# An adaLN, linear attention and GEGLU kernel: 1/den loads of another shape, two modulation products at other places, and the down projection's pairs interleaved

## The chip, the cores and the metric

One core of one Trainium2 chip. The metric is the device time of one execution in microseconds, the median of several runs; lower is better.

## The reference

The computation, cut to what matters (S = 2048 rows, D = 1024, 32 heads of 32, F = 3584; inputs in bf16):

```python
mod = (silu(c) @ w_mod).reshape(1, 6, 1, D)
sa, ca, ga, sb, cb, gb = ...                     # six rows of D
h = layernorm(x) * (1 + ca) + sa
q, k, v = heads(h @ wqkv)                        # [heads, S, 32]
phi = lambda t: where(t > 0, t + 1, exp(t)) + 1e-6
pq, pk = phi(q), phi(k)
kv = einsum('hsd,hse->hde', pk, v)
z = einsum('hsd->hd', pk)
num = einsum('hqd,hde->hqe', pq, kv)
den = einsum('hqd,hd->hq', pq, z)[..., None] + 1e-6
x = x + ga * (rows(num / den) @ wo)
h = layernorm(x) * (1 + cb) + sb
x = x + gb * ((gelu(h @ w_gate) * (h @ w_up)) @ w_down)
```

## The kernel before

Rows of x come in 16 chunks of 128 (`NCH`), in four super-groups of four chunks (`sg`, 512 rows); columns in eight groups of 128 (`g`), each holding four heads (`HPG = 4`, index k in the loads below). Every engine has one list of operations. PE (TensorE) and SP (the engine that issues nearly all DMAs) run theirs as written in the code; between two marks, from the startup to the first chunks of the wo stage, a planner (`reorder`) sorts the lists of VectorE (DVE), ScalarE (ACT) and GpSimd (POOL) by costs and due times. Waits are placed from what each operation reads and writes. SP's DMAs go round robin over eight lanes, and each DMA waits for the one eight before it.

The stages, in the order of PE:

- To about 127 us: q and k of h = LN(x), and phi of both.
- 127 to 191 us: 24 **m tiles** (`m_tile`), three of 342 columns or less for each group g, form pk^T against h; their results are transposed by DMA (`m_t`, tiles mb to mtb, L703) and multiplied by wv (`kv_prod`, L913), which gives each head's kv. The table `HOOK` says what is put on PE and SP behind which tile: `modp` = `mod_pass` (the products that turn the rows of sb and cb into one row each, `mod_rows`, and their store and reload as the columns sbT and cbT), `den0` and `den1` = `den` (pq against z, two super-groups each, four matmuls of 32 columns side by side, L1240, then reciprocal and a store to DRAM), `w0`, `w1` = `w2_pair` (kv times wo, 64 x 64 tiles, L1201), `gbr` = `gb_rows` (the row of gb), `rb...` = `rb_load`, `ps...` = `pq_scale`.
- 191 to 257 us, the **wo stage**: for each chunk 16 matmuls of pq against W2 (L1283), then x + the result and the second layernorm; ln2's rows are transposed by DMA (`T2`).
- 241 to 603 us: the FFN's gate and up products in 28 units, by a seven-product (Strassen-Winograd) scheme; their result goes to DRAM (`scr_y`).
- 599 to 778 us: the **down projection**, eight pairs of chunks (`d_pair0`, `d_pair`) by the same scheme, and the tail.

**1/den.** `scr_rd` holds 1/den in DRAM as [sg, h, k, g, 256]: h is a half of 256 rows. `rb_load` (L1255 to L1264) spreads it over partitions into `RB[sg % 2]`, two buffers: partitions 32k to 32k + 31 get head k's values. For each (sg, h) it issues four DMAs, one for each k, each from one row of 8 KB, repeated for 32 partitions. `pq_scale` (L1269 to L1274) multiplies pq in place, two g at a time on DVE; each multiply waits for all four DMAs. The chunks of (sg, h) wait for their multiplies. rb0 is loaded behind m tile 17, rb2.0 behind tile 23, rb1 and rb2.1 at the start of the wo stage, rb3 between its chunks (the table `SLOT`).

**A pair of the down projection.** For chunks ca and ca + 1 the products P1 to P7 have 14 matmuls each. P1 and P2 take y (`ya`, loaded from `scr_y` by `y_in`, two DMAs for each pair) and w_down (`wd`) as they are, in bf16; the others take sums of y (`d_s`, written to `sb` on DVE) and of w_down (`d_t`, `dt`, `dh`), in fp32. A pair uses four PSUM banks b0 to b0 + 3, and pairs alternate between b0 = 0 and 4. `d_cp` and `d_ecp` copy a bank to another bank or to the tile `DE` (ACT); `d_add` adds `DE` to a bank (DVE); `evac` multiplies by gb, adds x (`xq`, loaded by `x_in`) and stores the output. `hooks(i)` places further loads and sums after the products. For pairs 1 to 7 the order is P1, P5, P6, P2, P7, P3, P4:

```python
for k in (1, 5, 6, 2, 7, 3, 4):
    ...
    d_prod(ca, b0, k)
    if k == 1:   d_cp(b0 + 2, b0, "dpcp")
    elif k == 5: d_ecp(b0 + 3); d_s(ca, 2)
    elif k == 6: d_add(b0 + 1, b0 + 2); d_s(ca, 3); y_next(0)
    elif k == 2: evac(*parts[0])
    elif k == 7: d_add(b0 + 3, b0 + 2); d_s(ca, 4); y_next(1); evac(*parts[3])
```

Of the kernel before, what the change touches and what calls it, by code (L numbers as in the profile page):

```python
# [8 lines left out]
ALU = mybir.AluOpType  # L9
# [321 lines left out]
def bass_adaLN_cond__linear_attn_block__geglu_ffn__prompt_kernel(  # L331
# [18 lines left out]
    with ExitStack() as es:  # L350
# [449 lines left out]

        def gb_hilo(j):
            acc, rng = GA_[j]
            sch.op(A, lambda e: e.activation(HLG[:, j, 0, :], acc[:, :], ACTF.Copy), rd=rng, wr=r_hlg(j, 0), note=f"mhi{6 + j}")
            sch.op(V, lambda e: e.tensor_tensor(HLG[:, j, 1, :], acc[:, :], HLG[:, j, 0, :], ALU.subtract), rd=rng + r_hlg(j, 0), wr=r_hlg(j, 1), note=f"mlo{6 + j}")
# [3 lines left out]
        def gb_rows():  # L808
            mod_rows(((0, 2, 5, lambda j, h: (HLG[:, j, h, :], r_hlg(j, h))),))
            o_gb[0] = mod_store(2, 5, MRG, [(OFF_TMP + 4096, OFF_TMP + 5120, "mrg")], 2)  # L810
# [384 lines left out]

        def w2_pair(i, b0=4):
            for hf in range(2):
                for r in range(2):
                    for h in range(2):
                        b, g = b0 + 2 * r + hf, 2 * i + h  # L1200
                        sch.op(T, lambda e, b=b, g=g, h=h, r=r, hf=hf: e.matmul(ps_all[64 * h:64 * h + 64, b * 512:(b + 1) * 512], KVT[64 * r:64 * r + 64, g, 0:64],  # L1201
                               WO[64 * r:64 * r + 64, g, hf * 512:(hf + 1) * 512], start=True, stop=True),
                               rd=r_kvt(g, g + 1) + r_wo(g, hf * 512, (hf + 1) * 512), pwr=pr(b), note=f"w2 {i}.{hf}", overwrite_ok=True)
            for r in range(2):
                b, g = b0 + 2 * r, 2 * i + r
                w_, p_ = W2[:, g, :], ps_all[:, b * 512:(b + 2) * 512]
                eng = V if i > 1 and r else A
                sch.op(eng, lambda e, w_=w_, p_=p_, eng=eng: e.activation(w_, p_, ACTF.Copy) if eng == A else e.tensor_copy(w_, p_),
                       prd=pr(b) + pr(b + 1), wr=r_w(OFF_WK, "w2", g), note=f"w2cp{g}")
# [15 lines left out]
        def mod_pass():  # L1225
            assert mdone[0] >= 48 and not late
            mod_rows(((2, 4, 5, hl_src),))
            o_r = mod_store(4, 5, MROW[1], r_2k(OFF_ROW + 2048, "mrow1"), 1)
            for dst, nt, a0 in ((SBT, "sbT", 0), (CBT, "cbT", 2)):
                sch.dma(Q, lambda e, dst=dst, a0=a0: e.dma_start(dst[:, :], scr_row[1, a0:a0 + 2, :].rearrange("a (b p) -> p (a b)", p=P)),  # L1230
                        wr=r_sm(nt), deps=[o_r], note=nt)
# [21 lines left out]
        rb_ops = {}  # L1253

        def rb_load(sg, hs=(0, 1)):  # L1255
            i = sg % 2
            for h in hs:
                made = []
                for k in range(HPG):
                    made.append(sch.dma(Q, lambda e, h=h, k=k: e.dma_start(  # L1260
                        RB[i][32 * k:32 * (k + 1), h, :, :].rearrange("p a b -> p (a b)"),
                        scr_rd[sg, h, k:k + 1, :, :].rearrange("k g t -> k (g t)").to_broadcast([32, NG * HW])),
                        wr=r_rb(i, h) if k == 0 else (), deps=made[0].deps if k else [o_rd[sg // 2]], note=f"rb{sg}.{h}.{k}"))
                rb_ops[sg, h] = made  # L1264
# [3 lines left out]
        def pq_scale(sg, h, gs):  # L1268
            i, t0 = sg % 2, h * HW  # L1269
            for g0, g1 in gs:  # L1270
                ap = PQ[sg][:, g0:g1, t0:t0 + HW]
                rng = r_pq(sg, g0, g1, t0, t0 + HW)
                sch.op(V, lambda e, ap=ap, i=i, h=h, g0=g0, g1=g1: e.tensor_tensor(ap, ap, RB[i][:, h, g0:g1, :], ALU.mult),
                       rd=rng + r_rb(i, h, g0, g1), wr=rng, deps=rb_ops[sg, h], note=f"pqs{sg}.{h}.{g0}")  # L1274
# [3 lines left out]
        def wo_mm(c_, b0, gs):  # L1278
# [9 lines left out]
            if gs[-1] == NG - 1:  # L1288
# [13 lines left out]
        HOOK = {0: "ga", 6: "kv0", 10: "kv1", 11: "w0", 13: "kv2", 15: "modp kv3 z32", 16: "den0", 17: "w1 rb0.0 rb0.1", 18: "",  # L1302
                19: "kv4", 20: "den1 ps0.0", 21: "gbr", 22: "ps0.1", 23: "rb2.0"}
        st = {}

        def hook_run(f):
            if f[:2] == "kv":
                kv_prod(int(f[2:]), 4)
            elif f == "ga":
                ga_pass()  # L1310
            elif f == "gbr":
                assert mdone[0] == 64
                gb_rows()
            elif f == "modp":
                mod_pass()
            elif f == "z32":
                z32()
            elif f[:3] == "den":
                st[int(f[3:])] = den(int(f[3:]), 5)
                st[int(f[3:])]()  # L1320
            elif f[:2] == "ps":
                pq_scale(int(f[2]), int(f[4]), GH[0] + GH[1])
            elif f[:2] == "rb":
                rb_load(int(f[2]), (int(f[4]),))
            elif f[0] == "w":
                w2_pair(int(f[1:]))
# [328 lines left out]
        def d_prod(ca, b0, k, own=None, js=None):  # L1655
            b = b0 + {1: 0, 2: 0, 5: 3, 6: 2, 7: 2, 4: 2, 3: 1}[k] if own is None else own
# [3 lines left out]
            for j in js:  # L1660
# [11 lines left out]
                o = sch.op(T, lambda e, l_=l_, r_=r_, j=j, dst=dst: e.matmul(dst, l_[:, 0, :], r_, start=(k in (1, 5) or own is not None) and j == js[0], stop=j == js[-1], skip_group_check=True),  # L1672
# [48 lines left out]

        def d_pair(i, hook):
# [8 lines left out]
            for k in (1, 5, 6, 2, 7, 3, 4):  # L1731
                if last and k == 3:
                    d_prod(ca, b0, 3, None, range(6, NDJ))
                    evac_part(*parts[1])
                    continue
                d_prod(ca, b0, k)
                if k == 1:
                    d_cp(b0 + 2, b0, "dpcp")
                elif k == 5:
                    d_ecp(b0 + 3)  # L1740
                    d_s(ca, 2)
                elif k == 6:
                    d_add(b0 + 1, b0 + 2)
                    d_s(ca, 3)
                    y_next(0)
                elif k == 2:
                    evac(*parts[0])
                elif k == 7:
                    d_add(b0 + 3, b0 + 2)
                    d_s(ca, 4)  # L1750
                    y_next(1)
                    evac(*parts[3])
# [131 lines left out]
        def hooks(i):  # L1884
            def hook(k):
                more = i + 1 < 2 * CPG
                if i == 1:
                    if k == 1:
                        d_t(2, 5)
                        d_t(2, 6)  # L1890
                    if k in (6, 2, 7):
                        d_t(4, {6: 4, 2: 5, 7: 6}[k])
                    if k in (6, 7):
                        n = 1 if k == 6 else 2
                        evac(*parts_of(0)[n])
                        x_in(1, n)
                else:
                    if k == 1:
                        x_in(i, 0, 3, 1)
                    elif k == 5:  # L1900
                        x_in(i, 2)
                    if not more and k in (5, 6):
                        for q in {5: (0, 1), 6: (2,)}[k]:
                            t_gb(q)
            return hook

        d_pair0(hook0)
        for i in range(1, 2 * CPG):
            d_pair(i, hooks(i))
# [75 lines left out]
```

## Time and profile before

| what | us |
|---|---|
| median of three runs (782.70 to 783.98) | 782.91 |
| span of the profiled execution | 780.9 |
| FFN units, one every | 12.56 |
| down projection, one pair after pair 0 every | 22.03 |

The granted TensorE clock is 1.00 in every slice. "L1283" is line 1283 of the kernel; a line of a group names engine, operation and tiles (result<-inputs); in the timelines the columns are start, duration, engine, line, operation, tiles, shape and count, and in brackets the idle time before and what ended it. PE's busy time counts matmuls; weight loads (PEld) run beside them. A DMA's issue is SP's time to hand it over; "us to landing" is the time from issue until all of it is there.

The page's list of DMA issues for the transfers that the change touches (KB each, median us from issue to landing):

```
ya<-scr_y SPq DMA_DIRECT2D x14, 896.0 KB, 4.9
rb<-scr_rd SPq DMA_DIRECT2D x32, 256.0 KB, 6.0
xq<-scr_x SPq DMA_DIRECT2D x32, 128.0 KB, 2.6
scr_rd<-rdc SPq DMA_DIRECT2D x2, 128.0 KB, 3.8
mtb<-mb SPq DMA_TRANSPOSE x8, 4.9
```

### The profile page before, as it was taken

The page shows a single profiled execution, that of the slowest core. Times are in us where ns is not written, and L with a number is a line of the kernel's source. Part 1 is how long each engine was busy: PE and PEld are TensorE (multiplying, and loading weights), DVE is VectorE, ACT ScalarE, POOL GpSimd, SP SyncE. Part 2 cuts the span into 40 slices and gives each one's busy share as a digit, 9 for nine tenths or more (in the row PEclk, how much of TensorE's full clock was granted, in tenths as well). Part 3 has the DMA queues.
Part 4 walks back from the last instruction along what each step waited for, and adds up shares of the span by engine and source line. Part 5 has one row for each costly group of instructions (what it writes and reads, how often), then busy time and mean ns, then how long its engine had stood idle before and what let it go on. Part 6 is the DMA issues. An engine that isn't in the chain of part 4 may idle for free.

```text
span 780.9 us, 10753 instructions
## 1 busy us (share of the span) xinstructions
PE 770.2 (99%) x3825; PEld 496.2 (64%) x3883; DVE 645.9 (83%) x964; ACT 374.6 (48%) x629; POOL 47.5 (6%) x126
## 2 busy tenths in 40 slices
PE   8999999999999999999999999999999999999998
PEld 4444445666445667667676767667676576677766
DVE  6699988897899878787989888888989888676767
ACT  2497743242466487878755555555555211111111
POOL 2031300000321011100000000000000000000000
PEclk9999999999999999999999999999999999999999
DMA  9879749939999358867353865535356334443331
GB/s 284 256 167 252 158 91 215 255 80 196 203 287 231 82 138 212 230 175 215 99 145 108 250 211 172 148 96 161 97 147 221 111 127 139 144 141 114 126 125 60
DMA packets 196940, 130.22 MB, mean 167 GB/s; under 512 B 69516, under 2 KB 182420, under 8 KB 195864
## 3 DMA queue, kind: packets, MB, share of 16 engines
q1 hardware_dynamic: 196872, 129.55, 62.4%
q8 instruction: 30, 0.49, 0.3%
q14 instruction: 22, 0.18, 0.1%
q10 hardware_dynamic: 16, 0.00, 0.0%
HBM read 92.55 MB, written 23.35 MB: 148 GB/s over the span
## 4 chain that ended last, share of the span: by engine, by line
PE 95%; SPq 2%; DMA 1%; DVE 1%; issue 1%; ACT 0%; DVEq 0%; ACTq 0%
PE ps_all L1458 45%; PE ps_all L1672 21%; PE ps_all L895 7%; PE ps_all L934 7%; PE ps_all L1283 7%; PE ps_all L880 5%; PE ps_all L1593 1%; SPq L598 1%; DMA wmq<-in_w_mod_dram 1%; SPq L603 1%; DMA h1T<-xh 0%; PE ps_all L913 0%; PE ps_all L1201 0%; PE ps_all L1240 0%; DVE h1T L724 0%
## 5 line engine op out<-in xcount | busy, mean ns | idle before, releaser
L1458 PE MATMUL ps_all<-ss,tp 128*128 128x512 f32 x896 | 214.3, 396 | 0.0
L1458 PEld LDWEIGHTS ps_all<-ss,tp 128*128 128x128 f32 x896 | 168.3, 188 | 37.8 <-DVE ss L1413 0.2
L1672 PE MATMUL ps_all<-dt,sb 128*128 128x512 f32 x424 | 102.5, 398 | 0.0
L1481 ACT ACTIVATE ge<-ps_all 128x512 f32<-128x512 f32 x112 | 64.1, 597 | 73.8 <-DVE ps_all L1469 62.1
L1458 PE MATMUL ps_all<-h2a,wt 128*128 128x512 bf16 x421 | 95.7, 379 | 1.8
L1672 PEld LDWEIGHTS ps_all<-dt,sb 128*128 128x128 f32 x424 | 79.6, 188 | 18.5 <-DVE sb L1648 0.3
L1476 DVE TENSOR_TENSOR ps_all<-ps_all,es 128x512 f32<-128x512 f32 x54 | 37.6, 699 | 49.4 <-ACT es L1466 49.0
L1488 DVE TENSOR_TENSOR ys<-ge,ps_all 128x512 bf16<-128x512 f32 x112 | 74.4, 684 | 3.8 <-PE ps_all L1672 0.5
L1458 PEld LDWEIGHTS ps_all<-h2a,wt 128*128 128x128 bf16 x448 | 38.0, 98 | 57.3 <-ACT ps_all L1463 16.9
L1433 DVE TENSOR_TENSOR tp<-wt 128x1024 fp32r<-128x1024 bf16 x56 | 68.1, 1217 | 1.8 <-DMA wt<-in_B_w_up_dram 1.8
L1433 DVE TENSOR_TENSOR tp<-wt,tp 128x1024 fp32r<-128x1024 bf16 x56 | 68.2, 1218 | 0.0
L934 PE MATMUL ps_all<-h1T,wq 128*128 128x512 bf16 x256 | 56.7, 379 | 0.0
L880 PE MATMUL ps_all<-wk,h1T 128*128 128x512 bf16 x239 | 55.3, 379 | 1.1 <-DMA wk<-in_A_wqkv_dram 0.5
L1283 PE MATMUL ps_all<-w,pq 128*128 128x512 bf16 x249 | 55.7, 379 | 0.5 <-issue 0.2
L1458 PE MATMUL ps_all<-ar,tp 128*128 128x512 f32 x224 | 55.5, 390 | 0.0
L869 ACT ACTIVATE eb<-ps_all 128x512 f32<-128x512 f32 x64 | 36.3, 594 | 37.6 <-PE ps_all L880 16.0
L1672 PE MATMUL ps_all<-wd,ya 128*128 128x512 bf16 x199 | 47.5, 380 | 0.7
L1458 PEld LDWEIGHTS ps_all<-ar,tp 128*128 128x128 f32 x224 | 42.1, 188 | 8.9
L1463 ACT ACTIVATE ps_all<-ps_all 128x512 f32<-128x512 f32 x56 | 32.6, 582 | 26.8 <-PE ps_all L1458 26.5
L934 PEld LDWEIGHTS ps_all<-h1T,wq 128*128 128x128 bf16 x256 | 25.0, 98 | 30.0
L1283 PEld LDWEIGHTS ps_all<-w,pq 128*128 128x128 bf16 x256 | 24.6, 98 | 30.3 <-issue 1.1
L1643 ACT ACTIVATE sb<-ya 128x896 fp32r<-128x896 bf16 (+1 forms) x16 | 14.5, 913 | 58.8 <-PE ps_all L1672 58.8
(141 smaller groups left out, 976.3 us busy)
## 6 DMA issues: line engine op xcount, KB each, us to landing
wt<-in_B_w_gate_dram SPq DMA_DIRECT2D x28, 512.0 KB, 4.0
wt<-in_B_w_up_dram SPq DMA_DIRECT2D x28, 512.0 KB, 5.2
scr_y<-ys SPq DMA_DIRECT2D x28, 512.0 KB, 3.2
ya<-scr_y SPq DMA_DIRECT2D x14, 896.0 KB, 4.9
rb<-scr_rd SPq DMA_DIRECT2D x32, 256.0 KB, 6.0
wd<-in_B_w_down_dram SPq DMA_DIRECT2D x7, 1024.0 KB, 7.6
wmst<-in_w_mod_dram SPq DMA_DIRECT2D x6, 1024.0 KB, 6.2
wmq<-in_w_mod_dram SPq DMA_DIRECT2D x8, 512.0 KB, 7.5
```

What stands on the lines that cost most here:

```text
L869: sch.op(A, lambda e: e.activation(EB[i][:, :], PS(bank), ACTF.Exp), prd=pr(bank), wr=rng, note=f"{note}.exp")
L880: o = sch.op(T, lambda e, dc=dc: e.matmul(PS(bank), H1[sg][:, ci, dc, :], W_[:, dc, jg * 512:(jg + 1) * 512], start=(dc == 0), stop=(dc == ...
L895: o = sch.op(T, lambda e, c_=c_: e.matmul(PS(bank, 0, n), PK[c_][:, g * P:(g + 1) * P], xrow(c_, o_, o_ + n), start=(c_ == 0), stop=(c_ == ...
L934: o = sch.op(T, lambda e, dc=dc: e.matmul(PS(b), WQ[:, dc, qc * P:(qc + 1) * P], H1[sg][:, :, dc, :], start=(dc == 0), stop=(dc == NDC - 1 ...
L1283: last[half] = sch.op(T, lambda e, g=g, half=half: e.matmul(PS(b0 + half), PQ[sg][:, g, ci * P:(ci + 1) * P], W2[:, g, half * 512:(half + ...
L1433: sch.op(V, lambda e: e.tensor_tensor(TP[k][:], in0, in1 if k in (0, 2) else in1[:], ALU.subtract), rd=r0 + r1, wr=r_tp(k), deps=[x1_ops[7 ...
L1458: o = sch.op(T, lambda e, l_=l_, r_=r_, dc=dc: e.matmul(PS(b), l_, r_, start=fresh and dc == 0, stop=dc == ND2 - 1, skip_group_check=True) ...
L1463: sch.op(A, lambda e: e.activation(PS(BB + t), PS(BA + t), ACTF.Copy), prd=pr(BA + t), pwr=pr(BB + t), note="pcp")
L1476: sch.op(V, lambda e: e.tensor_tensor(PS(BC + t), PS(BC + t), ES[t][:, :], ALU.add), prd=pr(BC + t), rd=r_2k(OFF_ES[t], f"es{t}"), pwr=pr( ...
L1481: sch.op(A, lambda e: e.activation(GE[i][:, :], PS(b), ACTF.Gelu_apprx_tanh), prd=pr(b), wr=r_2k(OFF_GE[i], f"ge{i}"), note="gelu")
L1488: sch.op(V, lambda e: e.tensor_tensor(YS[s_][:, 2 * h:2 * h + 2, t, :], q(GE[i][:, :]), q(PS(b + 1)), ALU.mult), rd=r_2k(OFF_GE[i], f"ge{i ...
L1672: o = sch.op(T, lambda e, l_=l_, r_=r_, j=j, dst=dst: e.matmul(dst, l_[:, 0, :], r_, start=(k in (1, 5) or own is not None) and j == js[0] ...
```

## The change

It has three parts. **(1)** `rb_load` still issues four DMAs for each (sg, h), but each covers all 128 partitions and two g: its source is [k, 32 repeats, 512 values], its destination 128 partitions with 2 KB each. `pq_scale` waits only for the DMA of its own two g; three of its multiplies get an explicit wait on another operation (W2's copy of g 7, the last `mlo`). **(2)** `modp` moves from behind m tile 15 to behind tile 16, right ahead of `den0`, with `w1` right behind it (before: behind tile 17); `gbr` moves from tile 21 to tile 20, right behind `den1`. Their banks change from 5 to 2, 3 and 6. The loads of sbT and cbT leave `mod_pass` and are issued behind tile 22 (`sbl`). **(3)** In the down projection pairs 1 to 6 run P5, P6, P7, P2, then the next pair's P1 (`d_open`), then P3, P4; the last pair runs P5, P6, P2, P7, P3, P4. P7 of pairs 1 to 6 starts its own sum in bank b0 + 3, and `d_join` brings it together with the rest: one copy on ACT and one addition on DVE more for each of these pairs. The second load of the next pair's y and the loads of x move to other products.

```diff
@@ -798,16 +798,18 @@
                 sch.op(V, lambda e: e.scalar_tensor_tensor(acc[:, :], src, SILF[:, dc:dc + 1], acc[:, :], op0=ALU.mult, op1=ALU.add),
                        rd=rs_ + rng, wr=rng, note=f"macc{6 + j}.{dc}")
 
+        mlo7 = [None]
+
         def gb_hilo(j):
             acc, rng = GA_[j]
             sch.op(A, lambda e: e.activation(HLG[:, j, 0, :], acc[:, :], ACTF.Copy), rd=rng, wr=r_hlg(j, 0), note=f"mhi{6 + j}")
-            sch.op(V, lambda e: e.tensor_tensor(HLG[:, j, 1, :], acc[:, :], HLG[:, j, 0, :], ALU.subtract), rd=rng + r_hlg(j, 0), wr=r_hlg(j, 1), note=f"mlo{6 + j}")
+            mlo7[0] = sch.op(V, lambda e: e.tensor_tensor(HLG[:, j, 1, :], acc[:, :], HLG[:, j, 0, :], ALU.subtract), rd=rng + r_hlg(j, 0), wr=r_hlg(j, 1), note=f"mlo{6 + j}")
 
         o_gb = [None]
 
         def gb_rows():
-            mod_rows(((0, 2, 5, lambda j, h: (HLG[:, j, h, :], r_hlg(j, h))),))
-            o_gb[0] = mod_store(2, 5, MRG, [(OFF_TMP + 4096, OFF_TMP + 5120, "mrg")], 2)
+            mod_rows(((0, 2, 6, lambda j, h: (HLG[:, j, h, :], r_hlg(j, h))),))
+            o_gb[0] = mod_store(2, 6, MRG, [(OFF_TMP + 4096, OFF_TMP + 5120, "mrg")], 2)
 
         def mod_acc(k, dc):
             i, a = k % 2, k % 2
@@ -1193,6 +1195,8 @@
             sch.op(V, lambda e: e.tensor_tensor(Z32[:], BM32[:], ZCOLS[:, :].unsqueeze(2).to_broadcast([P, NG, NH]), ALU.mult),
                    rd=r_sm("bm32") + r_sm("zcols"), wr=r_sm("z32"), note="z32")
 
+        w2_ops = {}
+
         def w2_pair(i, b0=4):
             for hf in range(2):
                 for r in range(2):
@@ -1205,7 +1209,7 @@
                 b, g = b0 + 2 * r, 2 * i + r
                 w_, p_ = W2[:, g, :], ps_all[:, b * 512:(b + 2) * 512]
                 eng = V if i > 1 and r else A
-                sch.op(eng, lambda e, w_=w_, p_=p_, eng=eng: e.activation(w_, p_, ACTF.Copy) if eng == A else e.tensor_copy(w_, p_),
+                w2_ops[g] = sch.op(eng, lambda e, w_=w_, p_=p_, eng=eng: e.activation(w_, p_, ACTF.Copy) if eng == A else e.tensor_copy(w_, p_),
                        prd=pr(b) + pr(b + 1), wr=r_w(OFF_WK, "w2", g), note=f"w2cp{g}")
 
         def wofold(kc):
@@ -1224,11 +1228,15 @@
 
         def mod_pass():
             assert mdone[0] >= 48 and not late
-            mod_rows(((2, 4, 5, hl_src),))
-            o_r = mod_store(4, 5, MROW[1], r_2k(OFF_ROW + 2048, "mrow1"), 1)
+            mod_rows(((2, 4, 2, hl_src),))
+            o_sc[0] = mod_store(4, 2, MROW[1], r_2k(OFF_ROW + 2048, "mrow1"), 1)
+
+        o_sc = [None]
+
+        def mod_load():
             for dst, nt, a0 in ((SBT, "sbT", 0), (CBT, "cbT", 2)):
                 sch.dma(Q, lambda e, dst=dst, a0=a0: e.dma_start(dst[:, :], scr_row[1, a0:a0 + 2, :].rearrange("a (b p) -> p (a b)", p=P)),
-                        wr=r_sm(nt), deps=[o_r], note=nt)
+                        wr=r_sm(nt), deps=[o_sc[0]], note=nt)
 
         HW = SGW // 2
 
@@ -1250,18 +1258,15 @@
             return store
 
         o_rd = {}
-        rb_ops = {}
 
         def rb_load(sg, hs=(0, 1)):
             i = sg % 2
             for h in hs:
-                made = []
-                for k in range(HPG):
-                    made.append(sch.dma(Q, lambda e, h=h, k=k: e.dma_start(
-                        RB[i][32 * k:32 * (k + 1), h, :, :].rearrange("p a b -> p (a b)"),
-                        scr_rd[sg, h, k:k + 1, :, :].rearrange("k g t -> k (g t)").to_broadcast([32, NG * HW])),
-                        wr=r_rb(i, h) if k == 0 else (), deps=made[0].deps if k else [o_rd[sg // 2]], note=f"rb{sg}.{h}.{k}"))
-                rb_ops[sg, h] = made
+                for g0 in range(0, NG, 2):
+                    src = scr_rd[sg, h, :, g0:g0 + 2, :].rearrange("k g t -> k (g t)").unsqueeze(1).to_broadcast([HPG, P // HPG, 2 * HW])
+                    sch.dma(Q, lambda e, h=h, g0=g0, src=src: e.dma_start(
+                        RB[i][:, h, g0:g0 + 2, :].rearrange("p a b -> p (a b)"), src),
+                        wr=r_rb(i, h, g0, g0 + 2), deps=[o_rd[sg // 2]], note=f"rb{sg}.{h}.{g0}")
 
         GH = [((0, 2), (2, 4)), ((4, 6), (6, 8))]
 
@@ -1271,7 +1276,7 @@
                 ap = PQ[sg][:, g0:g1, t0:t0 + HW]
                 rng = r_pq(sg, g0, g1, t0, t0 + HW)
                 sch.op(V, lambda e, ap=ap, i=i, h=h, g0=g0, g1=g1: e.tensor_tensor(ap, ap, RB[i][:, h, g0:g1, :], ALU.mult),
-                       rd=rng + r_rb(i, h, g0, g1), wr=rng, deps=rb_ops[sg, h], note=f"pqs{sg}.{h}.{g0}")
+                       rd=rng + r_rb(i, h, g0, g1), wr=rng, deps={(2, 0, 0): [w2_ops.get(7)], (2, 0, 2): [w2_ops.get(7)], (0, 0, 2): [mlo7[0]]}.get((sg, h, g0), []), note=f"pqs{sg}.{h}.{g0}")
 
         x1_ops, s_ops = {}, {}
 
@@ -1299,8 +1304,8 @@
         wo_load(1)
         NWO = 5
         tiles = [(g, k) for g in range(4) for k in range(3)] + [(g, 0) for g in range(4, NG)] + [(g, k) for g in range(4, NG) for k in (1, 2)]
-        HOOK = {0: "ga", 6: "kv0", 10: "kv1", 11: "w0", 13: "kv2", 15: "modp kv3 z32", 16: "den0", 17: "w1 rb0.0 rb0.1", 18: "",
-                19: "kv4", 20: "den1 ps0.0", 21: "gbr", 22: "ps0.1", 23: "rb2.0"}
+        HOOK = {0: "ga", 6: "kv0", 10: "kv1", 11: "w0", 13: "kv2", 15: "kv3 z32", 16: "modp den0 w1", 17: "rb0.0 rb0.1", 18: "",
+                19: "kv4", 20: "den1 gbr ps0.0", 22: "sbl ps0.1", 23: "rb2.0"}
         st = {}
 
         def hook_run(f):
@@ -1313,10 +1318,12 @@
                 gb_rows()
             elif f == "modp":
                 mod_pass()
+            elif f == "sbl":
+                mod_load()
             elif f == "z32":
                 z32()
             elif f[:3] == "den":
-                st[int(f[3:])] = den(int(f[3:]), 5)
+                st[int(f[3:])] = den(int(f[3:]), (3, 5)[int(f[3:])])
                 st[int(f[3:])]()
             elif f[:2] == "ps":
                 pq_scale(int(f[2]), int(f[4]), GH[0] + GH[1])
@@ -1653,7 +1660,7 @@
                    note=f"dtsum gb{q}")
 
         def d_prod(ca, b0, k, own=None, js=None):
-            b = b0 + {1: 0, 2: 0, 5: 3, 6: 2, 7: 2, 4: 2, 3: 1}[k] if own is None else own
+            b = b0 + {1: 0, 2: 0, 5: 3, 6: 2, 7: 3 if 0 < ca < 4 * CPG - 2 else 2, 4: 2, 3: 1}[k] if own is None else own
             i = {1: None, 2: None, 5: 0, 6: 1, 7: 2, 3: 3, 4: 4}[k]
             o = None
             js = range(nj(ca)) if js is None else js
@@ -1669,7 +1676,7 @@
                     r_ = t_[:, 0]
                     if i == 4:
                         dst = dst.rearrange("p (h c) -> p h c", h=2)
-                o = sch.op(T, lambda e, l_=l_, r_=r_, j=j, dst=dst: e.matmul(dst, l_[:, 0, :], r_, start=(k in (1, 5) or own is not None) and j == js[0], stop=j == js[-1], skip_group_check=True),
+                o = sch.op(T, lambda e, l_=l_, r_=r_, j=j, dst=dst: e.matmul(dst, l_[:, 0, :], r_, start=(k in (1, 5) or k == 7 and 0 < ca < 4 * CPG - 2 or own is not None) and j == js[0], stop=j == js[-1], skip_group_check=True),
                            rd=rl + rr, pwr=(pr(b) if j == js[0] else ()), note=f"down P{k} c{ca} j{j}", overwrite_ok=True)
             pset_writer(b, o)
 
@@ -1719,6 +1726,16 @@
                     d_add(3, 2)
                 hook(k)
 
+        def d_join(b0):
+            d_ecp(b0 + 3)
+            d_add(b0 + 3, b0 + 1)
+            d_add(b0 + 2, b0 + 2)
+
+        def d_open(i):
+            b = i % 2 * 4
+            d_prod(2 * i, b, 1)
+            d_cp(b + 2, b, "dpcp")
+
         def d_pair(i, hook):
             ca, b0 = 2 * i, i % 2 * 4
             last = i == 2 * CPG - 1
@@ -1728,28 +1745,33 @@
                 if not last:
                     y_in(i + 1, r)
 
-            for k in (1, 5, 6, 2, 7, 3, 4):
+            for k in ((5, 6, 2, 7, 3, 4) if last else (5, 6, 7, 2, 1, 3, 4)):
                 if last and k == 3:
                     d_prod(ca, b0, 3, None, range(6, NDJ))
                     evac_part(*parts[1])
                     continue
+                if k == 1:
+                    d_open(i + 1)
+                    hook(k)
+                    continue
                 d_prod(ca, b0, k)
-                if k == 1:
-                    d_cp(b0 + 2, b0, "dpcp")
-                elif k == 5:
+                if k == 5:
                     d_ecp(b0 + 3)
                     d_s(ca, 2)
                 elif k == 6:
                     d_add(b0 + 1, b0 + 2)
                     d_s(ca, 3)
                     y_next(0)
+                elif k == 7:
+                    if last:
+                        d_add(b0 + 3, b0 + 2)
+                    else:
+                        d_join(b0)
+                    d_s(ca, 4)
+                    evac(*parts[3])
                 elif k == 2:
+                    y_next(1)
                     evac(*parts[0])
-                elif k == 7:
-                    d_add(b0 + 3, b0 + 2)
-                    d_s(ca, 4)
-                    y_next(1)
-                    evac(*parts[3])
                 elif k == 3:
                     evac(*parts[1])
                     d_s(ca + 2, 0)
@@ -1885,26 +1907,26 @@
             def hook(k):
                 more = i + 1 < 2 * CPG
                 if i == 1:
-                    if k == 1:
-                        d_t(2, 5)
-                        d_t(2, 6)
-                    if k in (6, 2, 7):
-                        d_t(4, {6: 4, 2: 5, 7: 6}[k])
-                    if k in (6, 7):
+                    if k in (6, 2):
                         n = 1 if k == 6 else 2
                         evac(*parts_of(0)[n])
                         x_in(1, n)
+                    if k in (6, 7, 2):
+                        d_t(4, {6: 4, 7: 5, 2: 6}[k])
                 else:
-                    if k == 1:
-                        x_in(i, 0, 3, 1)
-                    elif k == 5:
-                        x_in(i, 2)
+                    if k == 5:
+                        x_in(i, 1, 2)
                     if not more and k in (5, 6):
                         for q in {5: (0, 1), 6: (2,)}[k]:
                             t_gb(q)
+                if more and k in (1, 4):
+                    x_in(i + 1, 3 if k == 1 else 0)
             return hook
 
         d_pair0(hook0)
+        d_open(1)
+        d_t(2, 5)
+        d_t(2, 6)
         for i in range(1, 2 * CPG):
             d_pair(i, hooks(i))
 
```

## The prediction

> **What bounds the kernel now.** I read the page's first and fourth parts, then the busy time by stretches, then the timelines of TensorE, of the DMA-issuing engine SP and of VectorE around the three places that the diff touches, and the issue-to-landing times of single DMAs there.
>
> ```profile
> PE 770.2 (99%) x3825; PEld 496.2 (64%) x3883; DVE 645.9 (83%) x964; ACT 374.6 (48%) x629; POOL 47.5 (6%) x126
> ...
> PE 95%; SPq 2%; DMA 1%; DVE 1%; issue 1%; ACT 0%; DVEq 0%; ACTq 0%
> ```
>
> TensorE is busy for 770.2 of 780.9 us, and the chain of waits lies 95% on it. A gain is therefore TensorE time that disappears, and a loss is a wait that TensorE begins to feel. By stretches (columns: from and to, length, busy time and count of PE, weight loads, DVE, ACT, POOL, then granted clock, DMA share, GB/s):
>
> ```profile
> 191.00:242.00 51.00, 50.58 (x254) 23.05 (x258) 42.88 (x80) 29.03 (x43) 14.13 (x33) 1.00 1.06 232
> 197.00:209.00 12.00, 11.79 (x58) 5.47 (x57) 10.18 (x16) 3.84 (x6) 3.40 (x8) 1.00 1.02 221
> 667.50:689.60 22.10, 21.99 (x98) 15.73 (x98) 14.92 (x19) 3.09 (x4) 0.00 (x0) 1.00 0.40 130
> 686.00:689.00 3.00, 3.00 (x15) 2.50 (x14) 1.39 (x2) 0.00 (x0) 0.00 (x0) 1.00 0.82 310
> ```
>
> The reader should see two things. In the wo stage (191 to 242 us) TensorE is full and all sixteen DMA engines are full too (share 1.06): TensorE stays fed, but the queue has no room. In a pair of the down projection (667.5 to 689.6) TensorE has 0.11 us idle in 22.1.
>
> **Part 1, the 1/den loads.** 32 loads of 256 KB before and after, with the same number of issues on SP; only shape and waits change. Before, a load writes 32 partitions with rows of 8 KB, and its source's outermost level has 32 entries (a repeat). Afterwards the source's outermost level has four entries (k), then 32 repeats, then 2 KB rows. The packet counts of two short stretches tell how a load is dealt out, 179.9 to 181 us (one rb load's worth) and 168.5 to 172.5 us (one load of wmg and the 8 KB store of mrow):
>
> ```profile
> DMA packets 48, 0.26 MB, mean 238 GB/s; under 512 B 16, under 2 KB 16, under 8 KB 16
> ...
> DMA packets 536, 0.53 MB, mean 133 GB/s; under 512 B 20, under 2 KB 532, under 8 KB 536
> ...
> mtb<-mb SPq DMA_TRANSPOSE x1, 9.0
> ```
>
> In the first there are 32 packets of 8 KB and 16 of under 512 B: one completion write for each of sixteen engines, so two rows an engine. In the second 512 packets are wmg's, 4 are the store's four 2 KB rows, and of small packets there are 20, sixteen for wmg and four more: the store, the one transfer here whose outermost level has four entries, ran on four engines.
>
> ```profile
> 176.69 3.76 SPq L1260 DMA_DIRECT2D rb<-scr_rd  x8
> 180.55 1.23 SPq L703 DMA_TRANSPOSE mtb<-mb  x1
> ...
> 190.42 0.61 PE L913 MATMUL ps_all<-mtb,wv 128*128 128x128 bf16 x8
> ...
> 245.94 2.49 DVE L1273 TENSOR_TENSOR pq<-pq,rb 128x512 bf16<-128x512 bf16 x4
> ```
>
> Eight rb loads are issued from 176.69 us, the transpose of mb behind them at 180.55 to 181.78. The eight land 1.2 us apart, the last at 188.62; the transpose lands at 189.58 (9.0 after its issue, the third line above them), 0.96 later, in queue order; the kv product at 190.42 reads it. So what is issued on SP behind rb lands behind rb.
>
> Bounds of one load. *Sixteen engines:* eight 2 KB packets each; the x loads' 2 KB packets take 84 to 94 ns, so 0.7 to 0.75 us, under today's 1.2. *Four engines:* 32 packets each; by the same packets 2.7 to 3.0 us; by rates, one engine moves 310/16/0.82 = 23.6 GB/s in the fourth row above (64 KB in 2.8 us) and 221/16/1.02 = 13.5 in the second, while rb itself loads (4.85 us). I take four engines, as the mrow store, and 2.8 us: the rows are 2 KB, so the 2 KB packets are a nearer row than rb's 8 KB ones.
>
> The Trainium skill speaks against this change in the same way: "DMA: Bandwidth & Descriptors", section "Rules for kernel authors", says that an outermost dimension of fewer than 16 entries, a small leading repeat for instance, confines the whole DMA to at most that many engines. The mrow store agrees with its 4 completion writes; for a transfer with 4 entries on one side and 128 on the other no row here shows it. By it the sum is the one that follows; if it did not hold, the first rival's.
>
> What that costs. The DMA engines are saturated, so each load takes 2.8 − 1.2 = 1.6 us longer on the four that count, and 32 loads 51.2 us. First place felt: rb0's eight end at 177.2 + 1.85 + 8×2.8 = 201.5 in place of 188.6, the transpose lands at about 202.5, and the kv product waits 12 us from 190.42; kv products 6 and 7 and w2 follow it. Behind the loads on SP also stand the transposes of ln2's rows (T2), the x loads and the first weights. Last place: the last rb load landed at 242.37, and its last multiply starts at 247.75 (the row at 245.94), so 5.4 us were spare: 51.2 − 5.4 = 45.8, **taken as +46** (it contains the first 12). With 2.6 us per load +39, with 3.0 +52, with 4.85 +111. The waits that become narrower (each multiply for its own g part) gain nothing that TensorE feels: it stood idle 0.4 us in 51.
>
> **Part 2, modulation rows.** What is merged is TensorE's change of tile size:
>
> ```profile
> 169.11 1.47 PE L895 MATMUL ps_all<-xall,pk 128*128 128x342 bf16 x9
> 170.51 1.06 PE L1240 MATMUL ps_all<-pq,z 128*32 128x256 bf16 x32
> 171.50 0.90 PE L895 MATMUL ps_all<-xrow,pk 128*128 128x342 bf16 x5
> ```
>
> Starts within these rows: 342-column matmuls follow each other after 0.145 us, the last before the 32-wide tiles after 0.238; the four den matmuls of a group together take 0.11, the last group 0.31 − so about 0.09 on the way in and 0.10 out. Before there are five such stretches (mod rows, den0, w1, den1, gbr); after, den0 with its neighbours and den1 with gbr are two. Six switches go, of which I count five, since the w2 product's tiles differ in size from den's (64 against 32): 5×0.1 = **−0.5 us** (0 to −0.6). The two loads of sbT and cbT go from hook 15, where SP waited 169.7 to 172.2 for the row store, to hook 22; they are two SP issues of about 0.5 us each ahead of the transpose that lands at 194.22 for the kv product at 195.1: 0 to +0.1. Banks 2, 3 and 6 are taken from the m tiles' rotation at the same point of the order: 0.
>
> **Part 3, the down projection.** A pair is 28 bf16 matmuls at 0.216 us and 70 fp32 ones at 0.228: 22.0 us, against 22.03 from pair to pair. There is no wait at the boundary to remove: 0 gain. Added per pair: one d_add (0.70, DVE) and nothing on TensorE. DVE has 14.92 of 22.1 us busy, ACT 3.09, which covers it except in pair 1:
>
> ```profile
> 630.94 2.09 DVE L1648 TENSOR_TENSOR sb<-ya 128x896 fp32r<-128x896 bf16 x2
> 633.21 0.70 DVE L1695 TENSOR_TENSOR ps_all<-ps_all,de 128x512 f32<-128x512 f32 x1 [0.18 <-PE ps_all L1672]
> ...
> 647.06 2.09 DVE L1648 TENSOR_TENSOR sb<-ya,ya 128x896 fp32r<-128x896 bf16 x2
> ...
> 675.20 0.35 SPq L1571 DMA_DIRECT2D ya<-scr_y  x1
> ```
>
> From 630.94 to pair 2 DVE has no gap over 0.2 us. With 0.70 more and 0.18 idle recovered, pair 2's first sum half ends 648.15 + 0.5 = 648.6, where P5 of pair 2 would start at 648.58: with the semaphore's way, **+0.3 us** once (0 to 0.7). Later pairs: ya of the next pair is asked for at 675.20 here, 6.5 us into its pair, and the four such loads took 4.65 to 5.69; the next pair's P1, moved ahead of P3 and P4 of this one, needs it 12.6 us in: spare 0.4 to 1.4. I take 0 for each of six pairs, bounds 0 and 0.5. P7's own bank, the moved x loads and the last pair without P1: 0, their inputs are there before.
>
> **The sum.** 780.9 + 45.8 − 0.5 + 0.3 = 826.5 for the span; outside it lie 782.9 − 780.9 = 2.0 us, which carry over: **828.5 us**. Without the rb term: 782.7.
>
> **Rivals.**
>
> *The loads use all sixteen engines* (not slower than before), because the four entries and 32 repeats are dealt as 128 rows, or each load takes another four. For it: the destination has 128 partitions, and the mrow store had four entries on both its sides; the trace does not name the engine of a packet. Against it: the source's level is as short as the store's. Then 0.75 us a load, SP's queue is freer, TensorE has nothing to gain there, and modes and pair 1 give 780.9 − 0.5 + 0.3 + 2.0 = 782.7. From eight engines up (1.4 us a load) the loads cost at most 32×0.2 − 5.4 = 1 us, so that is the point from which the sign turns.
>
> *The opened pair waits* (slower a little). Loads on sixteen engines, but ya lands late in six pairs: 6×0.5 + 0.3 − 0.5 = +2.8, so 785.7. For it: 5.69 us was seen, and the four x loads now stand between other issues on SP; against it: 0.4 us spare even then.
>
> *Cleaner than thought* (faster). Sixteen engines, all six switches gone, no wait in pair 1, and the 0.4 us idle of the wo stage recovered: −0.6 − 0.4 = −1.0, 781.9, still inside what can't be told from no change. For more, TensorE time would have to vanish that no row here shows.
>
> **Chances and range.** A measurement of this kernel tells 0.2% (1.6 us) from no change. Four engines 0.76; sixteen, at 782.7, 0.18; the opened pair waits 0.03; cleaner 0.03, of which I leave 0.02 for a gain over 0.2% by something that no row shows. So slower 0.79, same 0.19, faster 0.02. The predicted time is the likeliest case's, 828.5. Its own range is 815 to 850, 2.4 to 3.5 us a load: below, a tenth under the 2 KB packets' 2.7; above, a third of the way from them to the 4.85 of the full stretch; some 0.12 of the case lies outside, mostly above. As that and the other cases together would leave out over 0.2, the range reaches to the sixteen-engine case: 781.5 to 850.
>
> **What would show it.** (1) Landings of successive rb loads 2.8 us apart, not 1.2 or 0.75, with 4 completion writes to 128 packets of 2 KB, and the DMA share of 191 to 242 far under 1. (2) The kv product after the m tiles starts near 202, released by the mb transpose, and the chunks before 14 wait for rb through VectorE. (3) One den stretch directly behind mod rows, about 0.5 us less between 166 and 186. (4) Pair 2's first P5 matmul at most 0.7 us late, pairs still 22.03 apart. The forecast is wrong if successive rb loads land under 1.4 us apart: then the time is the sum without them.

## The result, and the profile after

The changed kernel takes 831.32 us (median of four runs, 830.81 to 831.84); the kernel before took 782.81 us beside it (782.31 to 783.98). The ratio is 1.0616 (95% interval 1.0602 to 1.063), that is, 48.5 us slower. The profiled execution took 830.81 us with a span of 829.0.

The page of the changed kernel, first and fourth parts:

```profile
PE 791.0 (95%) x3883; PEld 500.6 (60%) x3883; DVE 649.4 (78%) x970; ACT 376.3 (45%) x635; POOL 43.8 (5%) x126
...
PE 82%; SPq 10%; DMA 6%; DVE 1%; issue 1%; DVEq 0%
```

The chain of waits lies outside TensorE for 18% of the span (5% before); SP's queue and DMAs stand there now. Two stretches by busy time, with the columns of before:

```profile
191.00:242.00 51.00, 33.47 (x154) 13.55 (x155) 21.85 (x38) 10.51 (x14) 4.96 (x16) 0.80 0.66 108
242.00:288.00 46.00, 36.80 (x134) 14.75 (x133) 29.09 (x51) 21.75 (x34) 6.58 (x18) 0.81 0.84 174
```

In 191 to 242 us TensorE is busy for 33.5 of 51 us (50.6 before), the DMA engines' share is 0.66 (1.06 before), and the granted clock is 0.80. So the sixteen DMA engines together do less, and yet everything waits for them. One rb load shows why: packet counts of the changed kernel from 225.4 to 227.9 us, with the queue's packets, MB and share of sixteen engines below:

```profile
DMA packets 128, 0.25 MB, mean 102 GB/s; under 512 B 4, under 2 KB 4, under 8 KB 128
...
q1 hardware_dynamic: 128, 0.25, 26.2%
```

Before there were 16 completion writes to a load, here there are 4, and the queue is busy for 26.2%, a quarter of sixteen engines, although further loads are queued behind. Successive loads complete at 225.45, 228.03 and 230.61: 2.58 us apart, in place of 1.2. What that does to SP, to the kv product and to the multiplies is seen in the timelines of SP, TensorE and VectorE:

```profile
203.44 34.44 SPq L1267 DMA_DIRECT2D rb<-scr_rd  x16
237.97 7.39 SPq L703 DMA_TRANSPOSE h2a<-xl  x1
...
200.99 1.01 PE L915 MATMUL ps_all<-mtb,wv 128*128 128x128 bf16 x8 [10.27 <-DMA mtb<-mb]
...
291.18 0.69 DVE L1278 TENSOR_TENSOR pq<-pq,rb 128x512 bf16<-128x512 bf16 x1 [2.42 <-DMA rb<-scr_rd]
293.73 0.69 DVE L1278 TENSOR_TENSOR pq<-pq,rb 128x512 bf16<-128x512 bf16 x1 [1.85 <-DMA rb<-scr_rd]
```

SP needs 34.44 us to issue the sixteen loads that it issued from 192.51 in 12.38 us before, and holds the first transpose of ln2's rows behind them. The kv product waits 10.27 us for the mb transpose that stands behind rb0. The last multiplies come as slowly as the loads, 2.55 us apart, and the last starts 293.73 − 247.75 = 45.98 us later than before. What the multiplies and TensorE wait for between 180 and 300 us (total, times, longest):

```profile
DVE pq L1278 <- DMA rb<-scr_rd: 41.9, 25, 2.8
PE ps_all L1288 <- DVE pq L1278: 15.2, 9, 4.2
PE ps_all L915 <- DMA mtb<-mb: 10.3, 1, 10.3
```

The span grew by 48.1 us. TensorE's idle time grew from 780.9 − 770.2 = 10.7 to 829.0 − 791.0 = 38.0 us, that is, by 27.3; the other 20.8 are busy time, for the same products. In the stretches with waits TensorE ran at a lower granted clock (0.80 and 0.81 above, 1.00 before); the last section shows what that does to a matmul.

### The profile page after: what moved, and what is told of

It is laid out like the page before. It is cut to its first block, busy times and chain, and to the rows that moved or that the text cites. A ratio compares the mean times of both kernels' runs of the same rounds, so it can differ in the third digit from the quotient of the medians.

```text
span 829.0 us, 10821 instructions
## 1 busy us (share of the span) xinstructions
PE 791.0 (95%) x3883; PEld 500.6 (60%) x3883; DVE 649.4 (78%) x970; ACT 376.3 (45%) x635; POOL 43.8 (5%) x126
## 4 chain that ended last, share of the span: by engine, by line
PE 82%; SPq 10%; DMA 6%; DVE 1%; issue 1%; DVEq 0%
PE ps_all L1465 42%; PE ps_all L1679 20%; PE ps_all L936 7%; PE ps_all L897 6%; PE ps_all L882 6%; SPq L703 4%; SPq L1267 4%; DMA rb<-scr_rd 3%; DMA mtb<-mb 1%; PE ps_all L1600 1%; SPq L598 1%; DMA wmq<-in_w_mod_dram 1%; SPq L603 1%; PE ps_all L1288 1%; SPq L592 0%
## 5 line engine op out<-in xcount | busy, mean ns | idle before, releaser
L1465 PE MATMUL ps_all<-h2a,wt 128*128 128x512 bf16 x448 | 103.3, 384 | 2.9 <-ACT ps_all L1470 2.6
L1288 PE MATMUL ps_all<-w,pq 128*128 128x512 bf16 x256 | 69.6, 433 | 15.3 <-DVE pq L1278 15.2
L1288 PEld LDWEIGHTS ps_all<-w,pq 128*128 128x128 bf16 x256 | 26.3, 108 | 57.3 <-DVE pq L1278 22.7
L1278 DVE TENSOR_TENSOR pq<-pq,rb 128x512 bf16<-128x512 bf16 x32 | 22.1, 692 | 42.1 <-DMA rb<-scr_rd 41.9
L1705 ACT ACTIVATE de<-ps_all 128x512 f32<-128x512 f32 x14 | 8.4, 597 | 90.3 <-PE ps_all L1679 90.3
```

Of the source, the lines that this page charges most:

```text
L1288: last[half] = sch.op(T, lambda e, g=g, half=half: e.matmul(PS(b0 + half), PQ[sg][:, g, ci * P:(ci + 1) * P], W2[:, g, half * 512:(half + ...
L1465: o = sch.op(T, lambda e, l_=l_, r_=r_, dc=dc: e.matmul(PS(b), l_, r_, start=fresh and dc == 0, stop=dc == ND2 - 1, skip_group_check=True) ...
```

## The experiments

Two helpers for reading them. The first 128 us vary by a microsecond or two from one execution to the next, long before anything that the change touches; so in this section stretches inside a profile are compared from the start of the last phi's exponential on ScalarE (127.66 us in the profile before) onwards. And "gelu" below is the first or last gelu of the FFN.

**The loads as before, the rest as changed.** `rb_load` and `pq_scale` of before:

```diff
-                for g0 in range(0, NG, 2):
-                    src = scr_rd[sg, h, :, g0:g0 + 2, :]...to_broadcast([HPG, P // HPG, 2 * HW])
+                for k in range(HPG):
+                    ... scr_rd[sg, h, k:k + 1, :, :]...to_broadcast([32, NG * HW])
```

> The changed kernel with the 1/den loads and the multiplies' waits of before; the modulation rows and the down projection stay as changed. Theory (the loads run on four DMA engines and carry the whole loss): 781.8 to 783.3 us, that is, all but 1 of the 48.5 us come back. Rival (the modulation rows or the interleaved pairs carry a part): a loss of more than 2 us stays, 785 us or more.

782.78 us against 782.72 for before, ratio 1.000 (0.9991 to 1.0009). The whole loss is in the loads.

**The new loads alone.** The kernel before with the changed `rb_load` and `pq_scale`.

> The kernel before with the new 1/den loads and nothing else of the change. Theory (four engines): 829 to 833 us, with the last 1/den multiply about 46 us later than before. Rival (the loss needs the moved modulation rows, which hold up the transposes): under 810 us.

831.69 us, ratio 1.0628 (1.0612 to 1.0645), as the changed kernel. The other two parts neither cause the loss nor soften it.

**The two outer levels exchanged.** Same bytes, rows, partitions and number of issues:

```diff
-...rearrange("k g t -> k (g t)").unsqueeze(1).to_broadcast([HPG, P // HPG, 2 * HW])
+...rearrange("k g t -> k (g t)").unsqueeze(0).to_broadcast([P // HPG, HPG, 2 * HW])
```

> The changed kernel with the two outer levels of each 1/den load's source exchanged: 32 repeats outermost, then the four heads, then the same rows of 2 KB to the same 128 partitions, with the same number of issues. The values of 1/den arrive at other heads' partitions; the work is otherwise the same. Theory (the outermost level's four entries set the number of DMA engines): about 0.75 us a load, 781.5 to 783.5 us. Rival (rows of 2 KB, or 128 partitions with a repeat, are slow by themselves): 2.5 us a load as in the changed kernel, about 831 us.

782.38 us, ratio 0.9994 (0.9985 to 1.0003). Rows of 2 KB over 128 partitions are not slow: only the order of the levels cost 49 us.

**Two, eight and sixteen entries outermost.** The source takes n of the sixteen 2 KB rows of (sg, h) and repeats each 128/n times:

```diff
-scr_rd[sg, h, :, g0:g0 + 2, :].rearrange("k g t -> k (g t)").unsqueeze(1).to_broadcast([HPG, P // HPG, 2 * HW])
+scr_rd[sg, h].rearrange("k (a b) t -> (k a) (b t)", b=2)[0:n, :].unsqueeze(1).to_broadcast([n, P // n, 2 * HW])
```

> The same with two entries outermost and 64 repeats; values at other heads. Theory: 5.16 us a load, so 32 x 2.58 = 83 us more than the changed kernel, 895 to 935 us, with two completion writes a load and a DMA share near 2/16 while they run. Rival (a fixed cost of each load): about 831 us.

> The changed kernel with eight entries in the outermost level of each 1/den load's source, 16 repeats below, the same 2 KB rows to the same 128 partitions; which rows of 1/den are read is altered, so the values arrive at other heads. Theory (as many DMA engines as outermost entries): 2.58 us a load at four make 1.29 at eight, 0.09 over the 1.2 of before, which 32 times is less than the 5.4 us that were spare: 781.5 to 784 us, and eight completion writes a load. Rival (fewer than sixteen engines is slow by a fixed cost of each load): about 831 us.

> The same with sixteen entries outermost and eight repeats; values at other heads, no stores added. Theory: no slower than 32 entries, about 0.65 us a load (SP's issue of one, as in the kernel with the repeats outermost) and 781.5 to 783.5 us. Rival (the 1.9 us of the kernel with four copies come from sixteen entries and not from its six added stores): 784 us or more.

| entries outermost | us between loads | median us | ratio to before (95%) |
|---|---|---|---|
| 2 | 5.13 | 906.06 | 1.1571 (1.1546 to 1.1596) |
| 4 (the change) | 2.58 | 831.32 | 1.0616 (1.0602 to 1.063) |
| 8 | 1.29 | 790.22 | 1.0085 (1.0064 to 1.0105) |
| 16 | 1.0 to 1.1 | 782.31 | 0.9993 (0.9983 to 1.0003) |
| 32 (levels exchanged) | 0.8 to 1.0 | 782.38 | 0.9994 (0.9985 to 1.0003) |

The loads of before came 1.2 to 1.3 us apart. The time of a load halves with each doubling of the entries from two to eight, and no further. The completion writes go along, here for two entries (251.2 to 256.3 us) and for eight (183.95 to 185.24 us), one load's worth each, and then for sixteen (179 to 181.5 us), where 330 data packets make 2.6 loads:

```profile
DMA packets 130, 0.26 MB, mean 51 GB/s; under 512 B 2, under 2 KB 2, under 8 KB 130
...
q1 hardware_dynamic: 130, 0.26, 13.2%
```

```profile
DMA packets 135, 0.26 MB, mean 202 GB/s; under 512 B 8, under 2 KB 8, under 8 KB 135
...
q1 hardware_dynamic: 135, 0.26, 52.1%
```

```profile
DMA packets 370, 0.68 MB, mean 270 GB/s; under 512 B 40, under 2 KB 40, under 8 KB 370
...
q1 hardware_dynamic: 370, 0.68, 105.5%
```

Shares of 13.2, 26.2 and 52.1% are two, four and eight of sixteen engines. With sixteen all engines are full. The expected 0.65 us a load is only SP's time to issue one: SP issues sixteen of these loads in 11.1 us, and they land over 15.9 us, 1.06 apart (1.01 in the first group of eight). Their 2 KB packets take about 131 ns each (median from 196 to 203 us) in place of 84 with two, four or eight entries; why, no run shows. With the levels exchanged a load lands every 0.99 us in the first group of eight and every 0.77 in the group of sixteen. The Trainium skill ("DMA: Bandwidth & Descriptors", section "Rules for kernel authors") states this limit for a short outermost level; the kernels with two, four and eight entries agree with it, and they show what the trace of before could not: the source's four entries decide although the destination has 128 partitions.

With eight entries the forecast for the time was missed: 790.2 where 781.5 to 784 stood. The load is 1.29 us as expected; the place was wrong. TensorE's waits of that kernel from 127 to 300 us (total, times, longest):

```profile
PE ps_all L915 <- DMA mtb<-mb: 3.0, 1, 3.0
PE ps_all L1465 <- ACT ps_all L1470: 0.5, 1, 0.5
PE ps_all L1465 <- DVE ss L1420: 0.5, 2, 0.3
```

The 5.4 us that I had reckoned with were spare at the last load only. The mb transpose behind rb0 had landed 0.8 us before its kv product, and now that product waits 3.0 us; from the last phi to the first x + result 5.6 us are lost, and 7.7 to the first gelu. Why the transpose lands 4 us behind the last rb0 load here, in place of 0.96, was not taken apart. SP needed 3.70 us to issue it (1.23 before), and in those 4 us the sixteen engines were nearly idle twice for about 1 us, so they were not simply full.

**Right values on sixteen and on eight engines.** 1/den is stored four times (or twice) in DRAM, so that (k, copy) gives 16 (or 8) entries:

```diff
-    scr_rd = nc.dram_tensor("scr_rd", [NSG, 2, HPG, NG, SGW // 2], f32).ap()
+    scr_rd = nc.dram_tensor("scr_rd", [NSG, 2, HPG, 4, NG, SGW // 2], f32).ap()
...
+    o_rd[pr_] = [sch.dma(Q, ... scr_rd[2 * pr_:2 * pr_ + 2, :, :, c]... RDC[:, :]) for c in range(4)]
...
+    src = scr_rd[sg, h, :, :, g0:g0 + 2, :].rearrange("k c g t -> (k c) (g t)").unsqueeze(1).to_broadcast([4 * HPG, P // HPG // 4, 2 * HW])
```

> The changed kernel with 1/den stored four times behind one another in DRAM, so that a load's source has 16 entries outermost and eight repeats below; the values are right. It costs six more stores of 128 KB in all. Theory: sixteen completion writes a load, about 0.75 us each, and 782 to 784 us, since the stores add at most six SP issues of 0.5 us. Rival (2 KB rows over 128 partitions are slow by themselves): about 831 us.

> The changed kernel with 1/den stored twice in DRAM, so that a load's source has eight entries outermost; the values are right, and two stores of 128 KB are added. Theory: loads of 1.29 us, hidden as before; the modulation rows save 0.3 us and the pairs 0.3 us, two SP issues cost at most 1: 781.8 to 783.5 us, not told from before. Rival (the added stores, not the entries, hold up the kv products, as in the kernel with four copies): 783.5 to 785 us.

Four copies: 784.61 us, ratio 1.0023 (1.0014 to 1.0032), a little above the expected range. TensorE's waits (127 to 300 us) say where:

```profile
PE ps_all L915 <- DMA mtb<-mb: 1.3, 2, 1.0
PE ps_all L915 <- issue: 1.2, 1, 1.2
```

The added stores stand on SP ahead of an mb transpose and of rb0, and the kv products wait 2.5 us for the transposes (the 1.2 us that the profile puts on "issue" end at 179.61, and the mb transpose landed at 179.52). Two copies: 794.09 us, ratio 1.0139 (1.0117 to 1.0162), above both theories; the kv product waits 4.0 us there, 1.0 more than with eight entries and no added stores. So no version with the right values on more engines beat the kernel before, and one that did would have had nothing to win: with sixteen entries and no stores added the loads come 1.0 to 1.1 us apart in place of 1.2 to 1.3, with the levels exchanged 0.8 to 1.0, and the time is the same both times.

**The pairs alone, and the modulation rows alone,** on the kernel before.

> The kernel before with the down projection's change alone. Theory (two changes between bf16 and fp32 matmuls fewer in each pair, 0.03 us apiece): a pair every 21.97 us in place of 22.04, 0.3 us less from the last unit's gelu to the last output, and a median within 0.2% of before, 781.9 to 783.0 us. Rival (the forecast's: one wait of 0.3 us in pair 1 and nothing gained): 0.3 us more over the same stretch.

> The kernel before with the modulation rows' change alone. Theory (fewer changes of tile size): the m tiles end 0.3 us earlier, seen from the last phi; 782.0 to 783.2 us. Open is whether the wo stage gives the 0.3 us back, as in the kernel with the loads of before: if that comes from VectorE's new order, it shows here too, and the first FFN gelu stands within 0.1 us of before; if it came from the multiplies' waits, the gelu is 0.3 us earlier.

Pairs alone: 782.90 us, ratio 1.0004 (0.9995 to 1.0013). Rows alone: 783.03 us, ratio 1.0006 (0.9998 to 1.0015). Neither can be told from before; the profiles say what happens below that. In the changed kernel the bf16 products of successive pairs start 21.98 us apart (before: 22.03):

```profile
706.52 6.22 PE L1679 MATMUL ps_all<-wd,ya 128*128 128x512 bf16 x28
...
728.50 6.22 PE L1679 MATMUL ps_all<-wd,ya 128*128 128x512 bf16 x28
...
750.47 6.22 PE L1679 MATMUL ps_all<-wd,ya 128*128 128x512 bf16 x28
```

P2 and the next P1 now lie together, so a pair has one stretch of bf16 in place of two. From the last gelu to the last output the changed kernel, and six others with its pairs, gain 0.32 to 0.35 us. With the pairs alone the gain was 0.01: one of the opened P1 waited 0.3 us for ya, which took 6.4 us to land there:

```profile
657.89 6.53 PE L1672 MATMUL ps_all<-wd,ya 128*128 128x512 bf16 x28
...
680.17 6.22 PE L1672 MATMUL ps_all<-wd,ya 128*128 128x512 bf16 x28
```

The stretch from 657.89 is 0.31 us longer than the one from 680.17. The kernel with four copies has such a wait too (0.34 us), the others none. With the rows alone the m tiles end 0.33 us earlier, and the wo stage gives 0.41 back in one place where a chunk waits for its multiply; with 32 or 16 entries outermost the 0.3 us stay. So the first of the two expected outcomes came: the first gelu stands within 0.1 us of before. I read it as TensorE catching up with its multiplies; whether the faster loads or the narrower waits of the kernels with 32 or 16 entries prevent it was not told apart.

## Why the prediction was right, step by step

**Four engines: shown.** The number of completion writes, the share, the exchanged levels and the row of 2, 4 and 8 all say so. The 831.3 us lie in the narrower range that was given for this case, 815 to 850, too.

**The size: right in sum, by two errors that cancel.** A load took 2.58 us, not 2.8. The forecast's own formula gives 32×(2.58 − 1.2) − 5.4 = 38.8 with that, and the last multiply was 46.0 late. The forecast took every load to cost the same 1.4 us more and everything else on the queue to stay as it was. Measured from a group's first issue to its last landing, the groups of 8, 16, 4 and 4 loads took 24.4, 45.7, 14.1 and 16.5 us, in place of 11.9, 22.6, 7.3 and 8.4: 50.4 us more in all, 6.3 over the 44.2 of 32×1.38. The last four are the furthest over (2.5 us); from 284 to 291 us, while they move, the weights' loads keep all sixteen engines full (share 1.01). The pauses between the groups grew by 2.0 us in all, as the next loads are issued behind multiplies and transposes that are late themselves, and the first load was issued 1.1 us earlier: together 7.2 us. That the load sized too long made up for these terms was luck.

**After the last multiply** the sum stopped, and 2.5 us more were lost: the first gelu is 45.99 late, the fifth 48.47, and from there to the end of the FFN it stays at 48.4 (the pairs then give 0.3 back). On VectorE a sum of the second layernorm's rows for the FFN's next product (`ss`) stands behind the multiply, and TensorE waits for it and then runs at half speed:

```profile
294.34 1.22 DVE L1420 TENSOR_TENSOR ss<-h2a,h2b 128x1024 fp32r<-128x1024 bf16 x1
...
297.94 2.50 PE L1465 MATMUL ps_all<-ss,tp 128*128 128x512 f32 x5 [2.43 <-DVE ss L1420]
...
298.00:302.90 4.90, 4.90 (x12) 2.98 (x13) 4.90 (x7) 0.87 (x2) 0.21 (x1) 0.50 0.66 186
```

The last line is the stretch from 298.0 to 302.9 us, with a granted clock of 0.50. That this half speed, and not the wait alone, makes the 2.5 us was read from the trace and not tried.

**First place felt.** The kv product: 202 forecast, 200.99 measured, released by the mb transpose, as said.

**Modulation rows.** −0.5 forecast, −0.3 measured from the last phi to the end of the m tiles in the kernels whose loads are as before or faster: the term was mis-sized. In the changed kernel itself it is +0.7, since `gbr`, now right behind `den1`, waits for the low part of gb's row, which VectorE computes at 182.61, behind a multiply that has waited 1.17 us for rb. I had priced that move at nothing:

```profile
183.35 0.28 PE L842 MATMUL ps_all<-hlg,ones 128*32 128x256 bf16 x2 [0.95 <-DVE hlg L806]
```

**The pairs.** "0 gain" was wrong by 0.33 us: I had taken the order of bf16 and fp32 products within a pair as free. The forecast wait of 0.3 us for VectorE in pair 1 came out at 0.07: the fp32 stretch after it is 16.40 us long against 16.33 in the next pairs (in the kernel with the loads of before). The ya wait stayed within its bounds, 0 or once 0.3 us.

**The rivals.** "All sixteen engines" fell, and its 0.75 us a load did not come either: 0.8 to 1.1 with sixteen engines. Its point of the sign, eight engines for at most 1 us, was wrong too: eight cost 7.7, and the loss ends between eight and sixteen, because spare time was counted at the last load where the transposes behind the first had less. Opened pairs that wait were seen, once each in two of nine such profiles. The 2.0 us outside the span came out as 1.8.

## What to carry to other kernels

Look at the order of a DMA's levels before its row size: the same number of bytes in rows of the same size took 0.8 to 5.13 us by the number of entries in the outermost level, and the count of completion writes in the profile shows it in one line. When a transfer gets slower, ask first what is queued behind it on its issuing engine and what each of these had to spare; the spare time of the last transfer says nothing about the first. The stage here, with its DMA share at 1 and TensorE full, gained nothing from faster loads and lost 7.7 us with loads of 1.29 in place of 1.2 us that ran on half of the engines.

## What the runs showed of the hardware

*SP itself is held up.* In the changed kernel the first few loads of a group are issued in 0.5 to 0.6 us each; from about the fifth on, an issue mostly takes 2.4 to 3 us, the time of one load on four engines (225.34 to 237.88: five issues, one every 2.5). So slow transfers hold up every later DMA of that engine.

*TensorE halves its speed after some pauses.* The kv product's matmuls after the pause of 10.6 us, and the chunk's behind it, run at half rate: 0.427 us for a 128x512 bf16 matmul in place of 0.216, for 3.7 us:

```profile
201.00:204.40 3.40, 3.40 (x15) 1.72 (x16) 0.45 (x2) 0.00 (x0) 0.00 (x0) 0.50 0.94 124
205.50:208.30 2.80, 2.80 (x29) 1.72 (x26) 1.92 (x5) 1.02 (x1) 0.00 (x0) 1.00 0.21 62
```

The granted clock is 0.50 in the first stretch and 1.00 in the second. Pauses (from one matmul's start to the next one's) of 2.8, 3.0, 4.0 and 10.6 us were followed by half speed at once in this profile; after one of 4.6 us it came 1.7 us later. Of three pauses of 1.9 us, one (at 237.7) was followed by half speed at once, and two (at 235.1, just ahead of it, and at 292.6) were not. So the length of a pause alone does not decide it. The Trainium skill ("TensorE: Matmul & The Clock Gate", Part 1) gives 426.7 ns for such a matmul at half rate, which agrees.

*Fewer changes between bf16 and fp32 matmuls:* a pair with two changes fewer takes 22.04 − 21.97 = 0.07 us less, about 0.03 for each if nothing else in the new order helps; no run tries a change alone.
